# Top-k attention with two MLPs: the weights w3 and w4 prepared first, key and value buffers planned, 28 low halves moved to GpSimd

## The chip, the cores and the metric

The kernel runs on one core of a Trainium2 chip. The metric is device time in microseconds (us), the median of several executions; a profile comes from one further execution.

The engines are named as in the profile: PE is the matrix engine (PEld its weight loads), DVE the vector engine, ACT the scalar engine, POOL GpSimd, and SP the engine whose queue (SPq) issues every DMA of this kernel.

## The reference

Shapes: q, k, v are 4 x 8 heads x 576 x 64 (float32); w_in 512 x 2048, w_out 2048 x 512, w1 and w2 512 x 1024, w3 1024 x 1024, w4 1024 x 512, all float64.

```python
scores = scale * np.matmul(q, k.transpose(0, 1, 3, 2))
kth = np.partition(scores, -32, axis=-1)[..., -32:-31]
scores = np.where(scores >= kth, scores, -1e9)
attn = softmax(scores)
x = np.matmul(attn, v)              # to 2304 tokens x 512
h = x @ w_in
g = np.where(h > 0.0, h, np.exp(np.minimum(h, 0.0)) - 1.0)
x = g @ w_out
out = ((x @ w1) * (x @ w2)) @ w3 @ w4
```

## The kernel before

**Tiling.** The 2304 tokens are cut into nine chunks of 256 (two tiles of 128 tokens). For every chunk `attention` makes x in buffer `XS` (three of them) out of four pairs of heads by two tiles; `mlp` then runs the chunk's matmuls in units: A (w_in, eight units), O (w_out, eight), Y (the evacuation between the MLPs), B (w1 and w2, eight) and D (the product of w3 and w4, one for each tile of tokens). The units of a chunk are written beside the attention of the next one.

**Attention.** For each tile and pair, q and k are split into a high and a low part (`QH`, `QL`; the key buffer `KT` holds both), the scores go through PSUM to `SS`, DVE finds the 32nd largest with four MAX8 and three MATCH_REPLACE8 for each head (L445, L447), ACT makes the exponentials, POOL the low halves (L471), the DMA transposes them (`PT`), PE multiplies by the values (L488), and a second transpose writes x (L510).

**Weights.** The raw words are float64. `load64` brings 128 x 512 words of 64 bits by one DMA and makes float32 of them: ACT (L539), DVE (L540), ACT (L541), POOL (L542). There are 16 such loads for w_in, 16 for w_out, 24 for w3 and w4, and 16 for w1 and w2, 72 in all. `prep_34` multiplies w3 by w4 in float32 (L686), so that D needs one product. Each weight is then normed and `convert` splits every piece into a high and a low float16 half. The high half is ACT's. The low half has a mode: "P" computes it on PE (L578, L579) and evacuates it by a DVE cast (L582); "D" computes it on DVE (L569). Before: w_in and w_out 16 P each, the w3-w4 product 8 D, w1 and w2 16 D.

**Homes.** There is no memory to spare, so raw words and the float32 pieces lie in buffers whose proper content comes later: `RAW8` (the w12 buffer) holds raw words for w_in and w_out, `RAW4` (half of it) those of w3 and w4; four pieces of w_in and four of w_out lie in the w34 buffer, so w34 cannot be filled before they are converted; pieces of w3 lie in `PP`, w4 in the upper half of the w12 buffer, and one piece of the product in the third x buffer.

**Key and value buffers.** `KT` has three and `VV` four, taken in turn. The first use of a batch and pair loads raw keys and splits them (ACT, POOL L358), then stores the split form to DRAM; later uses load that.

**The order.** Every instruction is handed to `Program.op` with an engine, a cost, the buffers that it reads and writes, and a priority. `emit` runs a list schedule once, with the priority (`PAR`, and an offset for each kind of unit and engine in `OFF`) less a multiple of the remaining critical path, and writes the instructions out in that order; the engines then run their queues in order. The order in which the `prep_` functions are called fixes which use of a shared buffer comes first: before, v's norm, w_in, w_out, w3 with w4, w1 with w2.

Of the kernel before, what the change touches and what calls it, by code (L numbers as in the profile page):

```python
# [8 lines left out]
F32 = mybir.dt.float32  # L9
# [24 lines left out]
PAR = dict(hv={}, lv={'wi': 16, 'wo': 16}, whole=(), cd={'wi': [0, 0], 'wo': [0, 0], 'w34': [8, 0], 'w12': [16, 0]}, pv=-577.81, pi=702.591, p34=-453.754, po=123.714, p12=822.408,   # L34
# [5 lines left out]
OFF = {":DVE": 13807, "A0:ACT": -12479, "A0:PE": 9089, "A0:POOL": 28926, "A1:ACT": 1887, "A1:PE": 1481, "A1:POOL": -6842, "A2:ACT": 12564, "A2:PE":  # L40
# [25 lines left out]
       -31006, "att8x:SP": -7783, "attsa:ACT": -35277, "attsa:PE": -26655, "attsk:ACT": -32653, "attsk:POOL": -8699, "attsk:SP": 1080, "attsm:ACT":  # L66
       65030, "attsm:POOL": 51251, "attsp:ACT": -17693, "attsp:POOL": 9395, "attsp:SP": 6312, "attsq:ACT": -8541, "attsq:POOL": 34851, "attsq:SP":
       1875, "attss:ACT": -12797, "attss:PE": -8952, "attst:DVE": 49668, "attsv:ACT": 31908, "attsv:DVE": 21919, "attsv:SP": 16024, "attsx:ACT":
# [3 lines left out]
       "w_in.c:PE": 10958, "w_in.n:DVE": -1688, "w_in.n:PE": 13297, "w_in:ACT": 7341, "w_in:DVE": -15198, "w_in:POOL": -10845, "w_in:SP": -55636,  # L72
       "w_out.c:ACT": -938, "w_out.c:DVE": -15709, "w_out.c:PE": -21068, "w_out.n:DVE": -35012, "w_out.n:PE": -11456, "w_out:ACT": 4851, "w_out:DVE":
       21248, "w_out:POOL": 24755, "w_out:SP": 20119, "w_v0:DVE": -51831, "w_v0:PE": 18056, "w_v0:SP": -23242, "w_v1:DVE": -16660, "w_v1:PE": 25930,
       "w_v1:SP": 54158, "w_v:DVE": -44716}


def conv_modes(n, d, g):

    m = ["P"] * n  # L80
    for k in range(d):
        m[k * n // d] = "D"
    free = [i for i in range(n) if m[i] == "P"]
    for k in range(min(g, len(free))):
        m[free[k * len(free) // g]] = "G"
    return m
# [7 lines left out]
class Program:  # L94
# [30 lines left out]
    def emit(self):  # L125
        n = len(self.ops)
        succ = [[] for _ in range(n)]
        miss = [0] * n
        for i, o in enumerate(self.ops):
            miss[i] = len(o[3])  # L130
            for d in o[3]:
                succ[d].append(i)
        cp = [0.0] * n
        for i in range(n - 1, -1, -1):
            e, c = self.ops[i][:2]
            cp[i] = c + max([cp[s] + (2050.0 if e == "SP" else LAT.get((e, self.ops[s][0]), 130.0)) for s in succ[i]], default=0.0)
        rank = [o[4] - PAR["cpw"] * cp[i] for i, o in enumerate(self.ops)]
# [4 lines left out]
        rt = [0.0] * n  # L142
        for i in range(n):
            if miss[i] == 0:
                heapq.heappush(wait[self.ops[i][0]], (0.0, i))
        order = []
        done, dma, locked = [], 0.0, 0.0
        for _ in range(n):
# [23 lines left out]
            if e == "SP":  # L172

                if len(done) >= 8:
                    t = max(t, done[-8])
                begin = max(dma, t + (1100.0 if lat < 500.0 else 1275.0))
                free[e] = max(t + lat, begin + 131.0) if lat > 1300.0 else t + lat
                dma = begin + cost
                end = dma + (1500.0 if lat > 1300.0 else 1900.0 if lat > 1000.0 else 1100.0)
                done.append(end)  # L180
            else:
                end = free[e] = t + cost
            for s in succ[i]:
                rt[s] = max(rt[s], end + (0.0 if e == "SP" else LAT.get((eng, self.ops[s][0]), 130.0)))
                miss[s] -= 1
                if miss[s] == 0:
                    heapq.heappush(wait[self.ops[s][0]], (rt[s], s))
        order.sort()
# [7 lines left out]
def kernel(ctx: ExitStack, tc: tile.TileContext, qd, kd, vd, vn, w_in, w_out, w1, w2, w3t, w4, out,  # L196
# [532 lines left out]
    def mlp(c, t0, n, dprev, pr0, span, hooks=None):  # L729
# [148 lines left out]
        if dp:  # L878
            seq.append(("Dp", dp.pop(0)))
# [108 lines left out]
```

## Time and profile before

| | |
|---|---|
| median of 3 runs | 1062.55 us (1062.33 to 1064.52) |
| time of the profiled execution | 1063.52 us |
| its span | 1061.7 us |
| busy PE / DVE / ACT / POOL | 978.0 / 888.4 / 826.1 / 695.2 us |
| mean granted PE clock | 0.974 |

The span is the time from the first to the last instruction of the profiled execution; what lies around it is 1.8 us. A busy share counts an engine as busy while one of its instructions runs; the idle time in front of an instruction is put down to what released it.

### The profile page before, as it was taken

What the parts mean: (1) busy time and instruction counts of PE and PEld (TensorE: products, weight loads), DVE (VectorE), ACT (ScalarE), POOL (GpSimd) and SP (SyncE); (2) the same over time, 40 slices, a digit from 0 to 9 for tenths busy, and PEclk for the clock granted to TensorE, in tenths of its full rate; (3) what the DMA queues carried; (4) which work ended last, traced back from release to release, by engine and by line L of the source; (5) the groups of instructions that cost most, each with busy time, mean ns of one, the idle gap of its engine ahead of it and who ended that gap; (6) DMA issues with size and microseconds to landing.
All of it is one profiled execution on the core that took longest, in us unless ns stands there. A gap on an engine that the chain in (4) does not pass through costs nothing.

```text
span 1061.7 us, 24618 instructions
## 1 busy us (share of the span) xinstructions
PE 978.0 (92%) x9132; PEld 776.7 (73%) x9132; DVE 888.4 (84%) x1968; ACT 826.1 (78%) x1521; POOL 695.2 (65%) x743
## 2 busy tenths in 40 slices
PE   3486998988899999999999999999999999999998
PEld 2334454777787788977888888788778968978875
DVE  4999998999999999999979999997999999710011
ACT  6899987898999767978887788899669877824512
POOL 4968665698478646965884587489457856833702
PEclk9598999999999999999999999999999999999999
DMA  9979997689456985488787536865862663320000
GB/s 356 397 223 289 304 273 171 192 209 236 118 161 153 238 192 120 90 193 212 187 227 174 147 76 176 221 188 140 179 154 65 138 151 70 57 51 21 1 20 20
DMA packets 255384, 174.97 MB, mean 165 GB/s; under 512 B 196640, under 2 KB 223264, under 8 KB 255264
## 3 DMA queue, kind: packets, MB, share of 16 engines
q1 hardware_dynamic: 255264, 173.41, 63.2%
q8 instruction: 71, 1.16, 0.5%
q14 instruction: 49, 0.40, 0.1%
HBM read 104.56 MB, written 21.61 MB: 119 GB/s over the span
## 4 chain that ended last, share of the span: by engine, by line
PE 33%; DVE 26%; ACT 16%; DMA 11%; POOL 6%; issue 6%; SPq 1%; DVEq 0%; ACTq 0%; POOLq 0%
DVE m L445 10%; DVE wk L447 8%; PE psR L826 2%; PE psR L827 2%; PE psR L828 2%; PE psY L784 2%; DMA raw<-kd 2%; PE psY L786 2%; PE psY L785 2%; DMA qr<-qd 2%; DMA pt<-pi 2%; PE psR L747 2%; PE psR L748 2%; PE psR L749 2%; PE psY L686 2%
## 5 line engine op out<-in xcount | busy, mean ns | idle before, releaser
L445 DVE MAX8 m<-wk 128x8 f32<-128x576 f32 x432 | 311.2, 746 | 0.8
L471 POOL TENSOR_TENSOR pi<-s,pi 128x576 f16<-128x576 f32 x144 | 185.9, 1298 | 80.3 <-ACT pi L470 57.1
L447 DVE MATCH_REPLACE8 wk<-m,wk 128x576 f32<-128x576 f32 x288 | 212.3, 740 | 0.0
L747 PE MATMUL psR<-x,win 128*128 128x256 f16 x576 | 157.2, 273 | 5.9 <-ACT t L768 5.6
L785 PE MATMUL psY<-g,wout 128*128 128x256 f16 x576 | 158.1, 275 | 3.3 <-POOL g L771 3.3
L784 PE MATMUL psY<-g,wout 128*128 128x256 f16 x576 | 158.5, 275 | 1.1 <-ACT g L770 1.1
L826 PE MATMUL psR<-x,w 128*128 128x256 f16 x576 | 158.0, 274 | 1.2 <-DVE t L846 0.9
L786 PE MATMUL psY<-g,wout 128*128 128x256 f16 x576 | 158.1, 274 | 0.0
L827 PE MATMUL psR<-x,w 128*128 128x256 f16 x576 | 157.6, 274 | 0.0
L828 PE MATMUL psR<-x,w 128*128 128x256 f16 x576 | 157.5, 273 | 0.0
L749 PE MATMUL psR<-x,win 128*128 128x256 f16 x576 | 157.0, 273 | 0.0
L748 PE MATMUL psR<-x,win 128*128 128x256 f16 x576 | 157.0, 273 | 0.0
L435 PE MATMUL psS<-kt,qh 128*128 128x288 f32 x320 | 111.7, 363 | 19.5 <-ACT s L437 18.4
L460 ACT ACTIVATE s<-s,m 128x576 f32<-128x576 f32 x144 | 108.6, 770 | 23.4 <-DVE m L445 23.2
L437 ACT ACTIVATE s<-psS 128x576 f32<-128x576 f32 (+1 forms) x160 | 102.9, 643 | 16.4 <-PE psS L435 9.7
L445 DVE MAX8 m<-s 128x8 f32<-128x576 f32 x144 | 104.5, 744 | 10.5 <-ACT s L437 10.3
L462 ACT ACTIVATE s<-s,ty 128x576 f32<-128x576 f32 x144 | 106.7, 769 | 4.4 <-POOL ty L456 4.4
L447 DVE MATCH_REPLACE8 wk<-m,s 128x576 f32<-128x576 f32 x144 | 106.1, 740 | 0.0
L470 ACT ACTIVATE pi<-s 128x576 f16<-128x576 f32 x144 | 95.0, 676 | 8.7 <-DMA pt<-pi 8.1
L769 POOL TENSOR_TENSOR t<-t,t 128x512 f32<-128x512 f32 x72 | 92.8, 1290 | 5.5 <-ACT t L768 3.8
L415 POOL TENSOR_TENSOR ql<-qr,qh 128x256 fp32r<-128x256 f32 x72 | 54.1, 752 | 60.8 <-ACT qh L414 57.0
L435 PE MATMUL psS<-kt,ql 128*128 128x288 f32 x320 | 93.4, 305 | 0.1
(155 smaller groups left out, 2382.6 us busy)
## 6 DMA issues: line engine op xcount, KB each, us to landing
kt<-kd SPq DMA_DIRECT2D x32, 576.0 KB, 4.6
vv<-vd SPq DMA_DIRECT2D x32, 455.0 KB, 4.6
qr<-qd SPq DMA_DIRECT2D x72, 128.0 KB, 3.0
raw<-kd SPq DMA_DIRECT2D x32, 288.0 KB, 3.8
kd<-kt SPq DMA_DIRECT2D x16, 576.0 KB, 4.6
w<-w_in SPq DMA_DIRECT2D x16, 512.0 KB, 5.9
w<-w_out SPq DMA_DIRECT2D x16, 512.0 KB, 6.9
w<-w3t SPq DMA_DIRECT2D x16, 512.0 KB, 5.5
```

The source lines that it names most:

```text
L435: T.matmul(psS[:, half, 0:288], lhsT=L[qs][:, hh], rhs=KT[kk][:, hh, half * 288:half * 288 + 288], start=li == 0, stop=li == 1)
L445: op("DVE", 665, lambda r=r, src=src, m8=m8, hh=hh: V.max(m8[:, hh, 8 * r:8 * r + 8], src), [skey], [mk], p1 + PAR["ot"] * STEP)
L447: op("DVE", 727, lambda r=r, src=src, w=w, m8=m8, hh=hh: V.match_replace(w, m8[:, hh, 8 * r:8 * r + 8], src, -3.0e38), [skey, mk], [k], p1 ...
L471: op("POOL", 1240, lambda Y=Y, PIs=PIs, hh=hh: G.tensor_tensor(PIs[:, hh, S:2 * S], Y[:, hh], PIs[:, hh, 0:S], op=OP.subtract), hks, [pk], ...
L747: T.matmul(o, lhsT=hi(W)[:, cs], rhs=X[:, 0, kd_, 0:N], start=kd_ == 0, stop=False)
L748: T.matmul(o, lhsT=hi(W)[:, cs], rhs=X[:, 1, kd_, 0:N], start=False, stop=False)
L784: T.matmul(o, lhsT=hi(W)[:, cs], rhs=rh, start=ft == 0 and m % 2 == 0, stop=False, skip_group_check=True)
L785: T.matmul(o, lhsT=hi(W)[:, cs], rhs=rl, start=False, stop=False, skip_group_check=True)
L786: T.matmul(o, lhsT=lo(W)[:, cs], rhs=rh, start=False, stop=ft == 15, skip_group_check=True)
L826: T.matmul(o, lhsT=hi(W)[:, cs], rhs=X[:, 0, kd_, 0:N], start=kd_ == 0, stop=False)
L827: T.matmul(o, lhsT=hi(W)[:, cs], rhs=X[:, 1, kd_, 0:N], start=False, stop=False)
L828: T.matmul(o, lhsT=lo(W)[:, cs], rhs=X[:, 0, kd_, 0:N], start=False, stop=kd_ == 3)
```

## The change

1. The calls are reordered: v's norm, w3 with w4, w_in, w_out, w1 with w2.
2. Raw words and pieces get other homes: raw w_in in the w_out buffer (eight places), raw w3, w4 and w_out in half of the w12 buffer (four places, one ring), v's norm in the upper half of w_in's buffer; four pieces of w_in and one of the product in the `T2` ring, three of w_out in the `GG` ring, both of which the A units write later.
3. A fourth mode "S" makes a low half with two POOL instructions: a scaling in place and a subtraction. `cd` sets 6 of w_in, 6 of w_out, all 8 of the product and 8 of w1 and w2 to S, 28 in all (the short description of the change says 34); 10 of w_in and 10 of w_out stay P and 8 of w1 and w2 stay D.
4. The key and value buffers are planned: a use that finds its content in a buffer loads nothing, the buffer whose next use is farthest is overwritten, and only what is loaded again is stored to DRAM. Odd chunks take the pairs of heads in reverse order.
5. The list schedule runs three times: once as before, then twice more with a rank made by a backward pass over the schedule just found (`fb=2`). All offsets in `OFF` have new values.

Two further options (`blag`, with `bprev` and `hold`) are added and switched off (`blag=0`).

```diff
-PAR = dict(hv={}, ... cd={'wi': [0, 0], 'wo': [0, 0], 'w34': [8, 0], 'w12': [16, 0]}, ...
+PAR = dict(fb=2, snake=1, blag=0, hv={}, ... cd={'wi': [0, 0, 6], 'wo': [0, 0, 6], 'w34': [0, 0, 8], 'w12': [8, 0, 8]}, ...
...
+    for z, mode in ((g, "G"), (s, "S")):
+        free = [i for i in range(n) if m[i] == "P"]
+        for k in range(min(z, len(free))):
+            m[free[k * len(free) // z]] = mode
...
+        cur = self.forward(succ, rank)
+        for _ in range(PAR["fb"]):
+            cur = self.forward(succ, self.backward(succ, cur[2]))
...
+    def pairs(c):
+        return range(4) if c % 2 == 0 or not PAR["snake"] else range(3, -1, -1)
+
+    def plan(n, uses):
...
+                if x in homes:
+                    steps.append((homes.index(x), "hit"))
+                    continue
+                far = [-1 if h in u else len(uses) + n - k if h is None else min([j for j in last[h] if j > i], default=len(uses)) for k, h in enumerate(homes)]
+                k = far.index(max(far))
+                homes[k] = x
+                if x in seen:
+                    again.add(x)
+                steps.append((k, "again" if x in seen else "first"))
+                seen.add(x)
...
     def att_loads(b, p, pr):
-        ks = nxt("k", NK)
-        if ("k", b, p) in seen:
+        ks, how = next(kplan)
+        if how == "hit":
+            return ks
+        if how == "again":
...
-        dma(KD[b, p], KT[ks].rearrange("p a s -> p (a s)").bitcast(F32), 128 * S * 8, [("k", ks)], [("kd", b, p)], pr + PAR["ost"] * STEP)
+        if (b, p) in kagain:
+            dma(KD[b, p], KT[ks].rearrange("p a s -> p (a s)").bitcast(F32), 128 * S * 8, [("k", ks)], [("kd", b, p)], pr + PAR["ost"] * STEP)
...
-    RAW8 = [r64(W12T, "w12", i) for i in range(8)]
-    RAW4 = RAW8[:4]
-    R12 = RAW8[6:]
+    RIN = [r64(WoutT, "wo", i) for i in range(8)]
+    RMID = [r64(W12T, "w12", i) for i in range(4)]
+    R12 = [r64(W12T, "w12", i) for i in (6, 7)]
...
-    HOMES = {"wi": [(W34[i], [("w34", i)]) for i in range(4)], "wo": [(W34[4 + i], [("w34", 4 + i)]) for i in range(4)], "w34": [(EX, ["ex"])], "w12": PPH[2:]}
+    HOMES = {"wi": T2H[:4], "wo": GGH, "w34": [T2H[4]], "w12": PPH[2:]}
...
-        if mode == "G":
-            op("ACT", 570, lambda: A.activation(st, st, AF.Copy, scale=s), [sk], skeys, pr)
+        if mode in "GS":
+            if mode == "G":
+                op("ACT", 570, lambda: A.activation(st, st, AF.Copy, scale=s), [sk], skeys, pr)
+            else:
+                op("POOL", 660, lambda: G.tensor_scalar(st, st, s, 1.0, op0=OP.mult, op1=OP.mult), [sk], skeys, pr)
             op("POOL", 1160, lambda: G.tensor_tensor(lo(W[i]), st, hi(W[i]), op=OP.subtract), [*skeys, (nm, i)], [(nm, i, "l")], pr)
...
     prep_v(0, PAR["pv"] * STEP)
+    prep_34(PAR["p34"] * STEP)
     prep_in(PAR["pi"] * STEP)
     prep_out(PAR["po"] * STEP)
-    prep_34(PAR["p34"] * STEP)
     st12 = prep_12(PAR["p12"] * STEP)
```

## Rows read from the trace of the kernel before

**Rows 1.** The page: busy time of each engine, share of the span, count

```profile
PE 978.0 (92%) x9132; PEld 776.7 (73%) x9132; DVE 888.4 (84%) x1968; ACT 826.1 (78%) x1521; POOL 695.2 (65%) x743
```

**Rows 2.** Busy time by stretch: start:end, length, PE, PEld, DVE, ACT, POOL, clock, DMA

```profile
0.00:195.00 195.00, 147.00 (x713) 78.06 (x714) 177.18 (x377) 164.30 (x292) 128.13 (x129) 0.89 0.93 280
195.00:270.00 75.00, 64.88 (x742) 56.46 (x740) 72.61 (x162) 67.99 (x127) 65.08 (x65) 0.98 0.84 214
270.00:925.00 655.00, 633.09 (x6519) 536.50 (x6517) 625.51 (x1394) 546.67 (x1021) 453.23 (x501) 0.99 0.64 154
925.00:1062.00 137.00, 132.99 (x1167) 105.64 (x1164) 13.14 (x38) 47.17 (x85) 48.81 (x50) 0.99 0.10 23
...
0.00:182.00 182.00, 134.00 (x675) 71.73 (x676) 164.18 (x349) 155.34 (x277) 122.80 (x122) 0.88 0.97 294
```

**Rows 3.** Timeline of PE at the first A unit: start, length, line

```profile
189.58 5.31 PE L686 MATMUL psY<-w,pp 128*128 128x512 f32 x12
194.73 0.27 PE L747 MATMUL psR<-x,win 128*128 128x256 f16 x1
```

**Rows 4.** The line of the last transpose of the first chunk's x: start and landing

```profile
L510 SPq DMA_TRANSPOSE x<-xt x1: 1167/1167/1167, 178.3 to 178.3; - x1
...
DMA to landing us min/median/max: 3.9/3.9/3.9
```

**Rows 5.** The chain that ended last, from 180 to 196 us: start, length, line

```profile
180.11 6.87 PE psY L686 x16
```

**Rows 6.** Low halves in mode P: L582 (shortest/median/longest ns, first to last start); busy time of L578, of L579

```profile
L582 DVE CAST win<-psY x16: 672/684/698, 55.4 to 78.3; 128x512 f16<-128x512 f32 x16
L582 DVE CAST wout<-psY x16: 667/682/692, 96.3 to 121.5; 128x512 f16<-128x512 f32 x16
...
0.00:195.00 195.00, 38.24 (x64) 11.14 (x64) 0.89 0.93 280
...
0.00:195.00 195.00, 12.85 (x32) 3.30 (x32) 0.89 0.93 280
```

**Rows 7.** Groups of DVE instructions by line, from 0 to 182 us: busy, mean ns

```profile
L445 DVE MAX8 m<-wk 128x8 f32<-128x576 f32 x60 | 43.9, 749 | 0.0
L540 DVE SCALAR_TENSOR_TENSOR w<-w,psR 128x512 int32<-128x512 int32 x56 | 37.5, 679 | 4.5 <-ACT psR L539 4.5
```

**Rows 8.** POOL lines: mode S's nearest, and the conversion of raw words

```profile
L762 POOL TENSOR_SCALAR t<-t,sc x72: 687/695/1284, 201.4 to 1001.5; 128x512 f32<-128x512 f32 x72
...
L771 POOL TENSOR_TENSOR g<-t,g x72: 1151/1163/1465, 205.7 to 1008.6; 128x512 f16<-128x512 f32 x72
...
L542 POOL TENSOR_TENSOR wout<-wout,w x12: 1288/1296/1307, 44.1 to 72.7; 128x512 int32<-128x512 int32 x12
```

**Rows 9.** SP's queue: first and last load of w1 and w2's sixteen

```profile
192.35 0.34 SPq L288 DMA_DIRECT2D pp<-w  x1
...
256.34 0.53 SPq L288 DMA_DIRECT2D pp<-w  x1
```

**Rows 10.** DVE: low halves in mode D and a top-k line; last the mean, 250 to 302

```profile
L569 DVE SCALAR_TENSOR_TENSOR w<-w,sc x21: 729/751/2698, 257.3 to 297.3; 128x512 f16<-128x512 f32 x21
...
L447 DVE MATCH_REPLACE8 wk<-m,wk x288: 730/741/756, 27.2 to 921.1; 128x576 f32<-128x576 f32 x144
...
L569 DVE SCALAR_TENSOR_TENSOR w<-w,sc 128x512 f16<-128x512 f32 x21 | 21.5, 1046 | 0.2
```

**Rows 11.** DMA issues by line: count, size, median us to landing

```profile
kt<-kd SPq DMA_DIRECT2D x32, 576.0 KB, 4.6
vv<-vd SPq DMA_DIRECT2D x32, 455.0 KB, 4.6
...
kd<-kt SPq DMA_DIRECT2D x16, 576.0 KB, 4.6
...
vd<-vv SPq DMA_DIRECT2D x16, 455.0 KB, 4.8
```

**Rows 12.** What PE waited for from 270 to 925 us: total, times, longest

```profile
PE psA L488 <- DMA pt<-pi: 7.4, 8, 2.2
```

More of the change, by code (lines that the diff above doesn't have):

```diff
@@ L123, in op, with forward @@
         self.groups.append(f"{self.tag}:{eng}")
-    def emit(self):
+    def forward(self, succ, rank):
         n = len(self.ops)
[L127 to L137, printed above, removed]
+        miss = [len(o[3]) for o in self.ops]
         engs = sorted({o[0] for o in self.ops})
@@ L142, in emit @@
         rt = [0.0] * n
+        fin = [0.0] * n
         for i in range(n):
@@ L182, in emit @@
                 end = free[e] = t + cost
+            fin[i] = end
             for s in succ[i]:
@@ L187, in emit, with backward @@
                     heapq.heappush(wait[self.ops[s][0]], (rt[s], s))
+        return max(free.values()), order, fin
+    def backward(self, succ, fin):
+        n = len(self.ops)
+        miss = [len(s) for s in succ]
+        engs = sorted({o[0] for o in self.ops})
+        free = {e: 0.0 for e in engs}
+        wait = {e: [] for e in engs}
+        ready = {e: [] for e in engs}
+        rt = [0.0] * n
+        late = [0.0] * n
+        for i in range(n):
+            if miss[i] == 0:
+                heapq.heappush(wait[self.ops[i][0]], (0.0, i))
+        for _ in range(n):
+            best = None
+            for e in engs:
+                if ready[e]:
+                    t = free[e]
+                elif wait[e]:
+                    t = max(free[e], wait[e][0][0])
+                else:
+                    continue
+                if best is None or t < best[0]:
+                    best = (t, e)
+            t, e = best
+            while wait[e] and wait[e][0][0] <= t:
+                _, i = heapq.heappop(wait[e])
+                heapq.heappush(ready[e], (-fin[i], i))
+            _, i = heapq.heappop(ready[e])
+            eng, cost, fn, deps, pr, lat, lk = self.ops[i]
+            free[e] = t + (max(cost, lat) if e == "SP" else cost)
+            end = free[e] + (1100.0 if e == "SP" else 0.0)
+            late[i] = -end
+            for d in deps:
+                de = self.ops[d][0]
+                rt[d] = max(rt[d], end + (900.0 if de == "SP" else LAT.get((de, eng), 130.0)))
+                miss[d] -= 1
+                if miss[d] == 0:
+                    heapq.heappush(wait[de], (rt[d], d))
+        return late
@@ new lines, in emit @@
+    def emit(self):
+        n = len(self.ops)
+        succ = [[] for _ in range(n)]
+        for i, o in enumerate(self.ops):
+            for d in o[3]:
+                succ[d].append(i)
+        cp = [0.0] * n
+        for i in range(n - 1, -1, -1):
+            e, c = self.ops[i][:2]
+            cp[i] = c + max([cp[s] + (2050.0 if e == "SP" else LAT.get((e, self.ops[s][0]), 130.0)) for s in succ[i]], default=0.0)
+        rank = [o[4] - PAR["cpw"] * cp[i] for i, o in enumerate(self.ops)]
+        cur = self.forward(succ, rank)
+        for _ in range(PAR["fb"]):
+            cur = self.forward(succ, self.backward(succ, cur[2]))
+        self.length, order, _ = cur
@@ L188, in emit @@
         order.sort()
-        self.length = max(free.values())
-        self.busy = {e: sum(o[1] for o in self.ops if o[0] == e) for e in engs}
+        self.busy = {e: sum(o[1] for o in self.ops if o[0] == e) for e in {o[0] for o in self.ops}}
         for _, i in order:
@@ L344 @@
     op("DVE", 135, consts, [], ["ident", ("xf", 0), *[(k, i) for k in ("v", "vl") for i in range(NV)]], -1e6)
+    def pairs(c):
+        return range(4) if c % 2 == 0 or not PAR["snake"] else range(3, -1, -1)
+    def plan(n, uses):
+        last, homes, seen, again, steps = {}, [None] * n, set(), set(), []
+        for i, u in enumerate(uses):
+            for x in u:
+                last.setdefault(x, []).append(i)
+        for i, u in enumerate(uses):
+            for x in u:
+                if x in homes:
+                    steps.append((homes.index(x), "hit"))
+                    continue
+                far = [-1 if h in u else len(uses) + n - k if h is None else min([j for j in last[h] if j > i], default=len(uses)) for k, h in enumerate(homes)]
[5 more added lines that the diff above has]
+                seen.add(x)
+        return iter(steps), again
+    starts = [sum(chunks[:i]) for i in range(len(chunks))]
+    kuse, vuse = [], []
+    for c_, n_ in enumerate(chunks):
+        for p_ in pairs(c_):
+            for t_ in range(starts[c_], starts[c_] + n_):
+                kuse.append([(b_, p_) for b_ in range(t_ * 128 // S, (t_ * 128 + 127) // S + 1)])
+            vuse.append([(b_, p_) for b_ in sorted({starts[c_] * 128 // S, ((starts[c_] + n_) * 128 - 1) // S})])
+    kplan, kagain = plan(NK, kuse)
+    vplan, vagain = plan(NV, vuse)
     def att_loads(b, p, pr):
-        ks = nxt("k", NK)
-        if ("k", b, p) in seen:
+        ks, how = next(kplan)
+        if how == "hit":
+            return ks
+        if how == "again":
             dma(KT[ks].rearrange("p a s -> p (a s)").bitcast(I32), KD[b, p].bitcast(I32), 128 * S * 8, [("kd", b, p)], [("k", ks)], pr)
             return ks
-        seen.add(("k", b, p))
         for hh in range(2):
@@ L400, in attention @@
         Kc, Vc = {}, {}
-        for pair in range(4):
-            base = (t0 * 8 + pair * n * 2 + PAR["a0"] * (c == 0) + PAR["a1"] * (c == 1)) * STEP
+        for at, pair in enumerate(pairs(c)):
             for t in range(n):
                 gt = t0 + t
-                idx = t0 * 8 + (pair * n + t) * 2
+                idx = t0 * 8 + (at * n + t) * 2
                 pr = (idx + PAR["a0"] * (c == 0) + PAR["a1"] * (c == 1)) * STEP
@@ L544 @@
     PPH = [(PP[:, 2 * i:2 * i + 2].rearrange("p a b -> p (a b)"), [("pp", 2 * i), ("pp", 2 * i + 1)]) for i in range(4)]
-    EX = XS[2].rearrange("p e k n -> p (e k n)").bitcast(F32)[:, 0:512]
-    HOMES = {"wi": [(W34[i], [("w34", i)]) for i in range(4)], "wo": [(W34[4 + i], [("w34", 4 + i)]) for i in range(4)], "w34": [(EX, ["ex"])], "w12": PPH[2:]}
+    T2H = [(T2[i], [("t", i)]) for i in range(NT2)]
+    GGH = [(GG[i], [("gh", i), ("gl", i)]) for i in range(NG)]
+    HOMES = {"wi": T2H[:4], "wo": GGH, "w34": [T2H[4]], "w12": PPH[2:]}
     def home(W, nm, i, n=16):
@@ L591, in prep_v @@
             if b == 0:
-                dst, keys = W12T[:, 2 * i:2 * i + 2].rearrange("p a b -> p (a b)")[:, 0:S], [("w12", 2 * i), ("w12", 2 * i + 1)]
+                dst, keys = WinT[:, 8 + 2 * i:10 + 2 * i].rearrange("p a b -> p (a b)")[:, 0:S], [("wi", 8 + 2 * i), ("wi", 9 + 2 * i)]
             else:
@@ L648, in prep_out @@
         P.tag = "w_out"
-        st = [stage(Wout, "wo", i, w_out[i * 128:i * 128 + 128, :], pr + i * PAR["pos"] * STEP, RAW8) for i in range(16)]
+        st = [stage(Wout, "wo", i, w_out[i * 128:i * 128 + 128, :], pr + i * PAR["pos"] * STEP, RMID) for i in range(16)]
         P.tag = "w_out.n"
@@ L669, in prep_34 @@
         for k in range(8):
-            load64(W4[k][0], W4[k][1], w4[k * 128:k * 128 + 128, :], None, pr, RAW4, "w34", "w4" in PAR["whole"])
+            load64(W4[k][0], W4[k][1], w4[k * 128:k * 128 + 128, :], None, pr, RMID, "wo", "w4" in PAR["whole"])
         def part(m):
@@ L726, in finish_12, with mlp @@
                 for i in range(16)]
-    def mlp(c, t0, n, dprev, pr0, span, hooks=None):
+    def mlp(c, t0, n, dprev, pr0, span, hooks=None, bprev=(), hold=False):
         xs, vb = c % NXS, batch(t0 + n)
@@ L877, in mlp @@
         dp = list(dprev)
+        seq += [("Bp", b) for b in bprev]
         if dp:
@@ L882, in mlp @@
             seq.append(("Dp", dp.pop(0)))
-        for j in range(8):
-            seq.append(("B", j))
+        if not hold:
+            for j in range(8):
+                seq.append(("B", j))
         for kind, i in seq:
             pr = pr_of(u)
-            c_ = c - (kind == 'Dp')
+            c_ = c - (kind in ("Dp", "Bp"))
             P.tag = f"{kind[0]}{c_ if c_ < 4 or c_ > len(chunks) - 3 else chr(115)}"
@@ L900, in mlp @@
                 i(pr)
-                u += 1
+                u += kind == "Dp"
             u += kind != "Y"
-        return [lambda pr, t=t: unitD(t, pr) for t in range(n)]
-    starts = [sum(chunks[:i]) for i in range(len(chunks))]
+        ds = [lambda pr, t=t: unitD(t, pr) for t in range(n)]
+        return (ds, [lambda pr, j=j: unitB(j, pr) for j in range(8)]) if hold else ds
     prep_v(0, PAR["pv"] * STEP)
+    prep_34(PAR["p34"] * STEP)
     prep_in(PAR["pi"] * STEP)
     prep_out(PAR["po"] * STEP)
-    prep_34(PAR["p34"] * STEP)
     st12 = prep_12(PAR["p12"] * STEP)
+    done12 = []
     def hooks(kind, i):
-        if kind == "Y":
+        if not done12 and (kind == "Bp" or kind == "Y" and not PAR["blag"]):
+            done12.append(1)
             for f in finish_12(st12, (PAR["p12"] + 16 * PAR["p12s"]) * STEP):
                 f()
-    dprev = []
+    dprev, bprev = [], ()
     for c, n in enumerate(chunks):
@@ L929 @@
             banks[:] = [0, 1] if c == 1 else [0, 1, 2]
-            dprev = mlp(c - 1, starts[c - 1], m, dprev, (starts[c] * 8 + PAR["lag0" if c == 1 else "lag"]) * STEP, m * 8 * STEP, hooks if c == 1 else None)
+            banks[:] = [0, 1] if c == 1 + PAR["blag"] else banks
+            hold = c == 1 and PAR["blag"] == 1
+            dprev = mlp(c - 1, starts[c - 1], m, dprev, (starts[c] * 8 + PAR["lag0" if c == 1 else "lag"]) * STEP, m * 8 * STEP, hooks if c < 3 else None, bprev, hold)
+            bprev = ()
+            if hold:
+                dprev, bprev = dprev
     c = len(chunks) - 1
```

48 lines of the change are left out of this document (22 added, 26 removed), and 56 rows, old and new, of the table OFF.

## The prediction

> **What bounds the kernel now.** I read the page first, then the busy time by stretch, then the places where one stretch ends. On the page PE is busy for 978.0 of 1061.7 us and DVE for 888.4 [rows 1]; a share over the whole span hides that the two are full at different times, so the stretches decide. Until 195 us PE works 147.0 of 195 us while DVE works 177.2: DVE is the fullest engine there. From 195 to 270 PE idles 10.1 us, from 270 to 925 it idles 21.9 of 655, and from 925 to the end 4.0 of 137, with DVE nearly idle [rows 2]. So the top-k is over 137 us before the end while PE still owes that much matmul time: PE is behind, and the end is *the start of the first A unit, plus PE's work from there, plus PE's idle time from there*. In numbers: 194.7 + 831 + 36 = 1061.7; the 831 is 978.0 less the 147.0 done by then. None of the 831 is preparation on PE that the change takes away: the P pieces were all done by 122 us [rows 6], and the other weights used D. The change can act on the first term and the third.
>
> What starts the first A unit? It begins at 194.7 directly behind the last product of w3 with w4 [rows 3], while the last piece of the first chunk's x was issued at 178.3 and landed 3.9 later, at 182.2 [rows 4]. So 12.5 us of the first term are PE finishing w3 times w4 in front of A; the rest is the pace of the first chunk's attention and the weights, which DVE, ACT and POOL share.
>
> **The change part by part.**
>
> *Order of the weights.* The product of w3 and w4 costs PE 128 half products; a dense run of 16 took 6.87 us, 0.43 each [rows 5], so 55 us in all. They ran up to 194 us, in front of A, and move to the first hundred microseconds, where PE idles for want of work. That alone is worth the 12.5 us to x's landing. More needs an earlier x: DVE loses 12 casts in front of it, 12 x 0.68 = 8.2 us [rows 6], so 174 at best.
>
> The condition is that w_in and w_out, now behind 24 more loads, are ready too: A reads w_in, and A's results go to the `GG` buffers that hold three pieces of w_out. I bound that from two sides. By load on the engines: what has to be done before A is nearly the list of before, 164.2 us of DVE, 155.3 of ACT and 122.8 of POOL by 182 [rows 2], less 8.2 on DVE, plus 20 S pieces on POOL. An S costs 0.70 + 1.16 = 1.86 us by the nearest rows [rows 8], so 37 us: DVE 156, ACT 155, POOL 160. All three come out alike; at the 90% that DVE held (164.2 / 182), POOL is through at 178, and at the 87% that POOL itself held in its busiest stretch (65.1 of 75 [rows 2]) at 184. By pace: the last of twelve pieces of w_out was finished at 74.0 [rows 8], the 28th load of the order w_in, w_out, so 2.64 each, 56 by 148; w_out's casts began 22 us behind that row and lasted 25 [rows 6]: 195. I take 180, nearer the first, since before the 28 loads by 74 shared their engines with loads of w4: DVE had handled 56 of all weights by 182 beside 60 MAX8 [rows 7]. That is **minus 14.7** (bounds minus 20.7 with A at 174, and 0 at 195).
>
> *P to S, 12 pieces.* On PE a P piece took (38.24 + 12.85) / 32 = 1.60 us [rows 6], so 19 us of PE work go. They lie before the first A, where PE idles 48 us: counted at **nothing**. If PE became full there, they would be worth those 19.
>
> *D to S, 16 pieces, and the stretch of w1 and w2.* DVE made its low halves in mode D at 257 to 300 us at a mean of 1.05 [rows 10]; 16 fewer, 17 us, leave a stretch in which DVE is full (72.6 of 75) and the first B waits on them. POOL gets 8 x 1.86 = 14.9 on top of 65.1 of 75: 80, five too many, unless w1 and w2 come earlier. They can: their first load was issued at 192.4 [rows 9], since w3's and w4's places were not free before; now these wait only for w_out's words. But ahead of A POOL is at 88% already, and up to 270 us it would have 128.1 + 65.1 + 28 x 1.86 = 245 us, 91%; only the second chunk's attention can give way. DVE's relief and POOL's burden cancel: **0** (bounds minus 10, PE's whole idle time in this stretch, and plus 9, POOL's 245 us at 88%).
>
> The median D took 0.75 us but the mean 1.05 and the longest 2.70, while 288 MATCH_REPLACE8 stayed within 730 to 756 ns beside the same POOL [rows 10]; so more POOL work costs the top-k nothing. The Trainium skill, "SBUF — State Buffer", section "Who interferes with whom", says that a DVE instruction with two SBUF inputs and a GpSimd instruction that reads SBUF contend for a shared read port, and the one that comes second is blocked for the whole instruction. The rows agree: D reads the piece and its high half. By the rule at its worst, with the top-k in that class too, 28 x 1.86 = 52 us of POOL would be taken from DVE and the forecast would become slower; the narrow MATCH_REPLACE8 row speaks against that, and I put it at 2 in 100, within the last rival.
>
> *Planned keys and values.* Stepping through `plan` over the nine chunks gives 12 loads of split keys for 32, 6 of values for 32, 12 stores of keys for 16 and 6 for 16 [rows 11]: 60 DMAs fewer and (20 + 4) x 0.576 + (26 + 10) x 0.455 = 30 MB less, on the queue in which the transposes stand. PE waited 7.4 us for these in 270 to 925 [rows 12]; the other 14 us of idle time there are waits on ACT and POOL, spread thin.
>
> *Three passes of the schedule, new offsets, reversed pairs.* No row prices an order. Beneath, 21.9 us of idle time can go; above, a worse order adds. Together with the loads I take **minus 5** for 270 to 925 (bounds minus 14 and plus 8).
>
> *The sum.* 1061.7 - 14.7 - 0 - 5 = 1042.0 for the span. The profiled execution took 1063.52, 1.8 more than its span, and stands 1.0 above the median of 1062.55; the median is 0.85 above that span. So **1043 us**, and 1028 to 1056 if the mechanism holds (first A at 174 to 190, the other terms between half their bounds).
>
> **The rivals.**
>
> *More than that* (1006 to 1028). PE's idle time after the first A, 36 us, is larger than the first term's gain, and DVE's 25 us of relief (17 + 8) lie where it was full. With the first A at 174 and the 36 cut to 18 the span is 1061.7 - 20.7 - 18 = 1023. Against it: 14 us of that idle time are waits of a microsecond or so each, which no single edit meets. Chance 0.13.
>
> *The start is hidden anyway* (1056 to 1064). The weights take the place of w3 times w4 as what A waits for, at the 195 of the slower pace: the first term gives nothing and the small ones 0 to minus 5. For it: w_out has four raw places instead of eight, in one ring with w3 and w4. Against it: the dense loads of before were paced by full engines, not by places. Chance 0.11.
>
> *Slower: POOL sets the start* (1064 to 1082). POOL's 160 us in front of A need 88% of the time; up to 182 it reached 67%. Its place is the last low halves of w_out, behind raw words, keys and probabilities in one queue; they hold back the `GG` buffers and so every A. At 80% POOL is through at 200, at 75% at 213: the first A is 5 to 18 late, and plus 0 to 2 for the rest. It decides from some 82% (160 / 195) down. Against it: POOL idled in front of A because ACT or DVE handed it work late, and some of its work by 182 is the second chunk's, which can wait. Chance 0.14.
>
> **How the numbers follow.** The forecast has 0.62. A change within 0.2% (1060.4 to 1064.7) is about what a measurement of this kernel cannot tell from none. Faster: 0.62 + 0.13 + 0.06 of the hidden start; within 0.2%: the other 0.05; slower 0.14. The range leaves out the slower rival (0.14) and the lower part of the better one (0.05): 1014 to 1063.
>
> **What would show it.** In the changed kernel's profile the w3-w4 products lie before 110 us; the first w_in matmul is at 174 to 190, not behind L686; L582 counts 20, the D line 8, a POOL scaling in place 28 at 0.7 us; kt<-kd counts 12 and vv<-vd 6; POOL is above 80% busy in front of the first A; PE is idle some 50 us before it and under 36 behind it; PE's busy time falls by 13 to 19 (13 at the dense rate of rows 5). The prediction is wrong if the first A stays at 190 or later, or if PE's idle time behind it moves by more than the start does: then the order was worth more than the starting point.

## The result, and the profile after

The changed kernel takes 1052.6 us (1052.16 to 1056.5, 4 runs), the kernel before 1062.4 beside it: a ratio of 0.9914 (0.9885 to 0.9942). It is faster by 9 us where 20 were forecast. The profiled execution took 1056.5 us with a span of 1054.7.

The page, the same rows as in [rows 1] and [rows 11], and the forty slices of PE:

```profile
PE 963.5 (91%) x9096; PEld 772.1 (73%) x9096; DVE 878.5 (83%) x1940; ACT 826.0 (78%) x1521; POOL 743.2 (70%) x799
PE   2598775697999999999999999999999999999998
...
kd<-kt SPq DMA_DIRECT2D x12, 576.0 KB, 4.2
kt<-kd SPq DMA_DIRECT2D x12, 576.0 KB, 3.9
...
vd<-vv SPq DMA_DIRECT2D x6, 455.0 KB, 4.7
vv<-vd SPq DMA_DIRECT2D x6, 455.0 KB, 4.5
```

PE lost 14.5 us of work, POOL gained 48, the DMAs are the counted ones, but DVE lost only 10 us of work where 25 were counted on. The products of w3 and w4 and the first A and B units (shortest/median/longest ns, first to last start), and the stretches up to the first A, to the first B, and to the end, as in [rows 2]:

```profile
L771 PE MATMUL psY<-w,pp x128: 590/592/1220, 40.8 to 120.5; 128*128 128x512 f32 x128
...
L832 PE MATMUL psR<-x,win x576: 269/273/421, 209.3 to 997.7; 128*128 128x256 f16 x192
...
L911 PE MATMUL psR<-x,w x576: 269/273/286, 283.1 to 1040.1; 128*128 128x256 f16 x192
...
0.00:209.30 209.30, 141.29 (x750) 76.92 (x751) 185.87 (x394) 180.90 (x322) 171.36 (x173) 0.90 0.88 267
209.30:283.10 73.80, 64.72 (x690) 57.77 (x688) 73.41 (x146) 63.83 (x119) 66.36 (x70) 0.91 0.48 107
283.10:1054.70 771.60, 757.51 (x7665) 637.37 (x7662) 619.27 (x1402) 581.22 (x1082) 505.45 (x558) 1.00 0.45 104
```

The products did move to the front and are over at 120 us. Yet the first A comes at 209.3, 14.6 us *later* than before, and the first B at 283.1, 13 later; PE idles 68.0 us ahead of A instead of 48. All of that is made good behind it. A cut at a fixed time shows where; PE's busy time up to 300 us and behind it, before, then after:

```profile
0.00:300.00 300.00, 238.34 (x1684) 157.53 (x1685) 279.36 (x598) 259.95 (x468) 207.07 (x207) 0.91 0.85 247
300.00:1061.70 761.70, 739.62 (x7450) 619.13 (x7448) 609.09 (x1371) 566.18 (x1055) 488.18 (x537) 1.00 0.55 132
```

```profile
0.00:300.00 300.00, 222.42 (x1614) 149.11 (x1615) 274.49 (x576) 259.83 (x468) 253.85 (x260) 0.91 0.78 221
300.00:1054.70 754.70, 741.10 (x7488) 622.95 (x7484) 604.05 (x1365) 566.12 (x1054) 489.31 (x540) 1.00 0.44 103
```

At 300 us both kernels have the same matmul work left, 739.6 and 741.1 us. The changed one has done 15.9 less by then, about what the change took away, and idled 15.9 more (77.6 for 61.7). So the start gained nothing, and the difference of 7 us between the two spans is idle time behind 300 us: 22.1 before, 13.6 after. The profiled execution of the changed kernel is the longest of its four, and the medians differ by 9.8; where the other 3 us lie, these two profiles do not show. Of PE's waits behind 300 us, those for transposes [rows 12] went from 7.4 to 1.0:

```profile
PE psS L516 <- ACT s L518: 2.0, 4, 1.1
...
PE psA L569 <- DMA pt<-pi: 1.0, 2, 0.6
```

### The profile page after: what moved, and what is told of

The parts are those of the page before. It is cut to its first block, busy times and chain, and to the rows that moved or that the text cites. A ratio compares the mean times of both kernels' runs of the same rounds, so it can differ in the third digit from the quotient of the medians.

```text
span 1054.7 us, 24477 instructions
## 1 busy us (share of the span) xinstructions
PE 963.5 (91%) x9096; PEld 772.1 (73%) x9096; DVE 878.5 (83%) x1940; ACT 826.0 (78%) x1521; POOL 743.2 (70%) x799
## 4 chain that ended last, share of the span: by engine, by line
PE 31%; DVE 29%; ACT 14%; POOL 6%; DMA 5%; issue 5%; SPq 0%; POOLq 0%; ACTq 0%; DVEq 0%
DVE m L526 13%; DVE wk L528 10%; PE psR L911 3%; PE psR L913 3%; PE psR L912 3%; PE psR L832 2%; PE psR L834 2%; PE psR L833 2%; PE psY L869 2%; PE psY L871 2%; PE psY L870 2%; DMA qr<-qd 2%; PE psS L516 2%; PE psA L569 2%; ACT s L543 2%
## 5 line engine op out<-in xcount | busy, mean ns | idle before, releaser
L551 ACT ACTIVATE pi<-s 128x576 f16<-128x576 f32 x144 | 97.3, 685 | 7.6 <-DMA pt<-pi 7.4
L516 PEld LDWEIGHTS psS<-kt,qh 128*128 128x128 f32 x320 | 62.9, 196 | 42.6 <-ACT s L518 21.4
```

Source lines behind the costliest of these rows:

```text
L516: T.matmul(psS[:, half, 0:288], lhsT=L[qs][:, hh], rhs=KT[kk][:, hh, half * 288:half * 288 + 288], start=li == 0, stop=li == 1)
```

## The experiments

Theories: the order of the weights and the modes set the start (the prediction's); the fewer transfers count; the three passes of the schedule count; or only the offsets, chosen for this one program. All ratios are to the kernel before.

**One part undone, planned anew.** Each time the schedule is made again with the offsets of the changed kernel. e1 puts the turn-taking `plan` of the kernel before in place of the new one, e4 restores the homes and order of the weights.

```diff
-    kplan, kagain = plan(NK, kuse)          # e1: buffers in turn, all stored
-PAR = dict(fb=2, ...                        # e2
+PAR = dict(fb=0, ...
-cd={'wi': [0, 0, 6], 'wo': [0, 0, 6], 'w34': [0, 0, 8], 'w12': [8, 0, 8]}   # e3
+cd={'wi': [0, 0], 'wo': [0, 0], 'w34': [8, 0], 'w12': [16, 0]}
-    prep_34(...)                            # e4: behind prep_out again
```

> The changed kernel with key and value buffers taken in turn again (32 loads of split keys, 32 of values, everything stored), all else as changed. If the fewer transfers are what moved the time, PE's waits for the transposed probabilities behind the first B, 1.0 us, go back to about 7 and the time to 1059 or more. If the order made the gain, the time stays within 2 us of 1052.6, since the order is planned anew around the added transfers.

> The changed kernel with one pass of the list schedule instead of three, offsets as changed. If the order is what moved the time, PE's idle time behind the first A, 23 us, grows to 36 or more and the time to 1062 or more. If transfers or the order of the weights made the gain, the time stays below 1056.

> The changed kernel with the modes of before: no low half by POOL, 32 by PE and 24 by DVE. If POOL's 52 us of low halves are what keeps the first A back at 209, it comes at 195 or sooner, and the time falls to 1045 or is at least no higher. If moving them to POOL helped, by 17 us less of DVE and 19 us less of PE in front of A, the first A comes later than 209 and the time is 1057 or more.

> The changed kernel with the weights in the order and the homes of before (w_in, w_out, then w3 and w4), modes and key buffers as changed. If w3 and w4 first is worth what the prediction said, some 15 us at the first A, the time is 1062 or more. If the order of the weights only moves the wait from PE to POOL, ACT and DVE, the time is within 4 us of 1052.6.

| | ratio (95%) | first A, first B | PE work, idle |
|---|---|---|---|
| changed kernel | 0.9914 (0.9885 to 0.9942) | 209, 283 | 963.5, 91.2 |
| e1, buffers in turn | 0.9958 (0.9935 to 0.9981) | 218, 284 | 966.1, 93.1 |
| e2, one pass | 1.0190 (1.0147 to 1.0233) | 229, 296 | 975.5, 110.0 |
| e3, modes of before | 1.0051 (1.0030 to 1.0072) | 180, 267 | 972.3, 89.2 |
| e4, weights as before | 1.0044 (1.0016 to 1.0072) | 193, 282 | 970.4, 97.6 |

The last two columns are those of the profiled execution alone; that of e3 is the shortest of eleven, 6.7 us below their median. Read by the ratios, e1, e3 and e4 would be worth 5 to 15 us each and e2 29, far more together than 9. e3 is the telling one: without POOL's low halves the first A comes at 180.0, as the prediction had it, and the kernel is slower than before. An early first A did not bring an early end.

**What an order alone does.** The same program with offsets moved at random by at most 1500:

```diff
-OFF = {":DVE": 19917, "A0:ACT": -36723, ...
+OFF = {each of them + randint(-1500, 1500)}
```

> The changed kernel with every offset of the schedule moved by a random amount of at most 1500 (they differ from those of before by some 15000), nothing else. It shows what a new order alone does to the time. If the offsets are a fine optimum for this one program, the time rises by 5 us or more, and the runs that undo one part and plan anew cannot be read below that; if it stays within 2 us, a loss of 7 us or more in those runs is due to the part undone.

> The changed kernel with another random draw of offsets moved by at most 1500. If the first draw, 0.9999, is typical, the ratio to before is 0.996 or more; if it was bad luck, 0.990 to 0.995.

> The kernel before, one pass, with its offsets moved by at most 1500 at random. If offsets found for one program are worth some 9 us in any kernel of this kind, the ratio is 1.005 to 1.015, and the changed kernel keeps its lead at drawn offsets. If the kernel before loses nothing, the changed kernel's gain is its offsets alone.

Measured: 0.9999 (0.9983 to 1.0014) and 1.0074 (1.0053 to 1.0094) for two draws of the changed kernel, 1.0043 (1.0019 to 1.0066) for one of the kernel before. A small push of the offsets costs the changed kernel 9 to 17 us, all of its gain and more, and the kernel before 5. It also moves the first A, from 209.3 to 190.7 and 190.9, with every part of the change in place. So e1, e3 and e4, which also run at offsets not chosen for them, cannot be read as the worth of the part undone: e3 and e4 lie between the two draws, and e1 on the good side of them. Only e2 is slower than both.

**One part alone, on the kernel before.**

```diff
+    def plan(n, uses): ...                  # e5: planned buffers, old sequence of pairs
+PAR = dict(fb=2, ...                        # e6, e12: forward() and backward(), old offsets
+tiny(... V.tensor_scalar ...)               # g2: e6 with the edit of e7, below
```

> The kernel before with only the planned key and value buffers (pairs in the old sequence), one pass, old offsets. If fewer transfers give the gain, PE's waits for transposes, 7.4 us from 270 to 925, fall to about 1 and the time to 1055. If the order does, the time is within 3 us of 1062.5.

> The kernel before with only the three passes of the schedule, old offsets. If the two backward passes give the gain, PE's idle time behind the first A falls from 36 to about 23 us and the time to 1052 to 1056. If the gain needs the offsets that were found for it, the time is 1060 or more.

> The kernel before with three passes of the schedule and the same random draw of offsets as e11 (1.0043 with one pass). If the passes gain at any offsets, the ratio is 0.992 to 0.998. If the gain of e6 (0.9916) was luck of its offsets, 1.000 or more.

> The kernel before with three passes of the schedule and the tiny tensor_tensor as tensor_scalar, the order as in e6. There these instructions take some 0.5 to 0.7 us each, 7 us in all, for 3 if they are not held up. If weights, modes and planned buffers add nothing at their chosen offsets, the ratio is 0.986 to 0.990, as for the changed kernel with the same mend (0.9857); if they add, 0.991 or more.

The planned buffers alone: 1.0789 (1.0747 to 1.0831), neither of the two outcomes named, with 140 us of PE idle time and 18.9 us of waits for transposes between 300 and 1060 us; why one pass places the planned loads so badly was not followed further. The passes alone: 0.9916 (0.9888 to 0.9943), the gain of the whole change; at drawn offsets 0.9901 (0.9881 to 0.9920), against 1.0043 for the same draw with one pass. With the edit of g2 0.9908 (0.9890 to 0.9927): DVE has 7 us less to do than in e6, and the time is the same. That lies between the two outcomes named, and is read below, beside e7. Here are e6 and e12, cut at 300 us:

```profile
0.00:300.00 300.00, 239.31 (x1693) 157.82 (x1694) 284.56 (x600) 261.77 (x471) 208.56 (x207) 0.97 0.85 248
300.00:1053.80 753.80, 736.02 (x7441) 617.18 (x7439) 606.88 (x1369) 562.64 (x1051) 486.24 (x536) 1.00 0.56 133
```

```profile
0.00:300.00 300.00, 239.46 (x1712) 158.51 (x1713) 283.58 (x604) 263.33 (x474) 209.75 (x209) 0.98 0.86 247
300.00:1047.10 747.10, 732.90 (x7423) 615.88 (x7420) 604.25 (x1365) 560.32 (x1048) 485.21 (x535) 1.00 0.55 135
```

They have 3.6 and 6.7 us less work left at 300 us than the kernel before, and 17.8 and 14.2 us of idle time behind it for 22.1. Together that is 7.9 us behind 300 us in e6, about what the changed kernel saves there (7.0), without a change of weights, modes or buffers; but only half of it is idle time. The 14.6 of e12 are too many: its profiled execution is the shortest of five, 5 us below their median.

**Transfers at the same order, and w1 and w2 held back.** f4 issues a transfer that nobody reads behind sixty of the loads of q, with the planner's input unchanged. e8 makes the loads of w1 and w2 wait for the first x and calls their preparation behind the first attention; its order is planned anew, with the offsets of the changed kernel.

```diff
+                    Q.dma_start(DUM[d % 4][:, 0:S], kd[d % 4, d % 8])           # f4
-        dma(st, src, 128 * 512 * 8, [], rk, pr)                                 # e8
+        dma(st, src, 128 * 512 * 8, [("xh", 0, k) for k in range(4)] if nm == "w12" else [], rk, pr)
-    st12 = prep_12(PAR["p12"] * STEP)
+    st12 = []
...
+        if c == 0:
+            st12 += prep_12(PAR["p12"] * STEP)
```

> The changed kernel in the same order with one more transfer of 288 KB (keys from DRAM to DRAM, into a scratch tensor that nothing reads) behind each load of q from the thirteenth on: 60 more DMAs, as many as the plan of the key and value buffers took away, with 17 MB read and 17 written. If transfers were worth the gain, PE's waits for transposes, 1.0 us, rise to 5 or more and the time by 4 us or more. If they lie beside other work, less than 2 us.

> The changed kernel with the sixteen loads of w1 and w2 held until the first chunk's x has landed. In the changed kernel they run at 105 to 207 us, in front of the first A, where before they ran at 192 to 256. If they are what keeps the first A back at 209, with 21 us on POOL, 20 on ACT and 11 on DVE, it comes at 195 or sooner; the first B, then behind them, at 285 or later, and the time is the same or up to 5 us more. If the low halves on POOL keep A back, A stays near 209.

f4: 0.9970 (0.9952 to 0.9988), 6 us more than the changed kernel; PE's waits for transposes behind 300 us are 3.0 for 1.0, its idle time there 17.6 for 13.6. The time moved as if transfers were worth the gain, the waits did not. Sixty transfers cost some 6 us, then (2 to 10 by the two intervals), though little of it shows as a wait. They are not the ones that the plan took away: those were 576 and 455 KB, between DRAM and SBUF; and each of the sixty also takes a place in SP's queue, which was not separated from its bytes. e8: 0.9970 (0.9949 to 0.9990); the first A comes at 189.2, the first B at 303.2. Holding the loads of w1 and w2 brings A forward by 20 us and puts B back by 20. But as in e3 the order is a new one, and the draws above bring A to 191 with these loads about where they were; so this does not show that the loads alone had pushed A back.

**Which engine sets the start.** The same instructions in the same order, some of them on 16 columns: the 28 scalings of mode S (f1), 26 of the MAX8 (f2), 26 of the exponentials (f3), planned as 16 to 17 us less for one engine each.

```diff
+ G.tensor_scalar(st[:, 0:16], st[:, 0:16], s, 1.0, op0=OP.mult, op1=OP.mult)      # f1
+ V.max(m8[:, hh, 8 * r:8 * r + 8], src[:, 0:z])                # f2: z = 16, tiles 6 to 18, r = 3
+ A.activation(Y[:, hh, 0:z], Y[:, hh, 0:z], AF.Exp, ...)       # f3: z = 16, tiles 6 to 18
```

> The changed kernel, same instructions in the same order, with the 28 scalings on POOL done on 16 columns instead of 512 (part of the scaling is left out): 28 x 0.6 = 17 us less of POOL, all between 130 and 302 us, 20 of them in front of the first A. If POOL sets the start, PE's idle time in the first 300 us, 77.6, falls by 8 or more and the time by 6 to 14 us. If DVE sets it, the time falls by less than 3 us, except for what DVE waits for POOL.

> The changed kernel, same instructions in the same order, with the last MAX8 of 26 rows of the top-k (tiles 6 to 18) on 16 of 576 scores (part of the top-k is left out): 26 x 0.6 = 16 us less of DVE, most of it between 100 and 260 us. If DVE sets the start, PE's idle time in the first 300 us falls by 8 or more and the time by 6 to 14 us. If POOL or ACT sets it, the time falls by less than 3 us.

> The changed kernel, same instructions in the same order, with 26 of the exponentials (tiles 6 to 18) on 16 of 576 columns (part of the exponentials is left out): 26 x 0.6 = 16 us less of ACT over the same stretch. If ACT sets the start, the time falls by 6 to 14 us; if DVE or POOL does, by less than 3 us. If all three engines share it, each of the three runs gives 2 to 6 us.

f1 0.9859 (0.9835 to 0.9883), f2 0.9874 (0.9852 to 0.9897), f3 0.9917 (0.9889 to 0.9945): 6, 4 and 0 us less than the changed kernel, the 4 only just clear of noise. The engines' busy time over the run fell by less than planned, 11.3 us on POOL (f1), 11.9 on DVE (f2), 9.9 on ACT (f3), and PE's idle time in the first 300 us by 3.6, 3.5 and not at all, where 8 or more had been named. The gain shows as work done by then: 734.9 (f1), 733.5 (f2) and 742.0 us (f3) are left at 300 us for 741.1.

The order was the same, but the three are not clean: DVE instructions with two inputs in SBUF (the memory that DVE and POOL work in) change their length from run to run. In f1 DVE's own busy time fell from 878.5 to 871.4 with no DVE instruction changed, and two instructions on 128 x 1 numbers make 6.4 of these 7.1 us; e7 below gains as much by mending them alone. So f1 shows no worth of POOL's work beyond them. In f2 and f3 the same two were short as well, but one low half of the values was long (timeline, start and length; the changed kernel, f2, f3):

```profile
234.78 0.98 DVE L467 SCALAR_TENSOR_TENSOR vv<-raw,sc,vv 128x640 f16<-128x640 f32 x1
...
230.64 7.15 DVE L467 SCALAR_TENSOR_TENSOR vv<-raw,sc,vv 128x640 f16<-128x640 f32 x1
...
239.24 6.27 DVE L467 SCALAR_TENSOR_TENSOR vv<-raw,sc,vv 128x640 f16<-128x640 f32 x1
```

There the two changes nearly cancel, and the 4 us of f2 speak for DVE's other work; ten us less of ACT gave nothing.

**The tiny instructions.** In the changed kernel two DVE operations on 128 x 1 numbers last four microseconds (timeline, start and length):

```profile
238.10 3.77 DVE L694 TENSOR_TENSOR sc<-sc 128x1 f32<-128x1 f32 x1
241.80 0.75 DVE L526 MAX8 m<-wk 128x8 f32<-128x576 f32 x1
242.47 0.14 DVE L695 RECIPROCAL sc<-sc 128x1 f32<-128x1 f32 x1
242.53 4.44 DVE L702 TENSOR_TENSOR sc<-sc 128x1 f32<-128x1 f32 x1
```

POOL was busy without a break beside them; these are its instructions beside the second one, which ended at 246.97, with the last but one of them:

```profile
242.63 1.16 POOL L856 TENSOR_TENSOR g<-t,g 128x512 f16<-128x512 f32 x1
243.75 1.28 POOL L552 TENSOR_TENSOR pi<-s,pi 128x576 f16<-128x576 f32 x1
244.99 0.74 POOL L498 TENSOR_TENSOR ql<-qr,qh 128x256 fp32r<-128x256 f32 x1
245.68 1.28 POOL L854 TENSOR_TENSOR t<-t,t 128x512 f32<-128x512 f32 x1
247.04 1.42 POOL L441 TENSOR_TENSOR kt<-raw,kt 64x576 fp32r<-64x576 f32 x1
```

e7 writes such lines with one column as a scalar operand; b1 also issues the scalings of mode S on ACT, at the same places.

```diff
-        tiny(lambda: V.tensor_tensor(phi, sv, r, op=OP.mult), ...       # e7, b1: eight such lines
+        tiny(lambda: V.tensor_scalar(phi, sv, r, None, op0=OP.mult), ...
-                op("POOL", 660, lambda: G.tensor_scalar(st, st, s, 1.0, op0=OP.mult, op1=OP.mult), ...    # b1
+                op("POOL", 660, lambda: A.activation(st, st, AF.Copy, scale=s), ...
```

> The changed kernel with its eight lines of tiny DVE tensor_tensor on two 128x1 columns in SBUF written as tensor_scalar with the second column as the scalar; the same order of instructions. Two of these took 3.77 and 4.44 us at 238 to 247 us, beside a POOL that is full. If they wait for POOL because they have two SBUF inputs, each becomes 0.2 us, DVE gains 8 us in front of the first B, which comes up to 7 earlier, and the time falls by 2 to 7 us. If something else stretched them, they stay long and the time is the same.

> The changed kernel with the tiny instructions as tensor_scalar and the 28 scalings issued on ACT, at their places in the order, instead of on POOL; everything is computed. If DVE and POOL set the start and ACT has room (16 us less of ACT gave nothing), the gains of 6 us each add in part, since both free the same DVE instructions: ratio to before 0.980 to 0.985. If ACT then becomes the bound, 28 x 0.6 = 17 us more on it, 0.986 or more.

e7: 0.9857 (0.9824 to 0.9891), 1050.1 us, the fastest version here that computes everything, beside 0.9914 for the changed kernel. The same two operations in e7, and in f1, with the POOL instructions beside them in f1:

```profile
244.49 0.20 DVE L694 TENSOR_SCALAR sc<-sc 128x1 f32<-128x1 f32 x1
245.28 0.14 DVE L695 RECIPROCAL sc<-sc 128x1 f32<-128x1 f32 x1
245.34 0.19 DVE L702 TENSOR_SCALAR sc<-sc 128x1 f32<-128x1 f32 x1
```

```profile
240.34 1.10 DVE L694 TENSOR_TENSOR sc<-sc 128x1 f32<-128x1 f32 x1
242.09 0.66 DVE L702 TENSOR_TENSOR sc<-sc 128x1 f32<-128x1 f32 x1
...
240.15 1.27 POOL L854 TENSOR_TENSOR t<-t,t 128x512 f32<-128x512 f32 x1
241.44 1.29 POOL L552 TENSOR_TENSOR pi<-s,pi 128x576 f16<-128x576 f32 x1
```

In f1 POOL is as full there as in the changed kernel (17.8 of the 18 us from 232 on in both), yet each of the two was held for one POOL instruction, not for several. How long such an instruction is held is thus a matter of how it falls between POOL's, and not of POOL's load alone. In e7 the two are short beside a busy POOL, but a low half of the values takes 5.63 us instead; over the run DVE's busy time fell by 7.7.

With the tiny instructions mended the changed kernel stands at 0.9857 and the kernel of before with three passes at 0.9908 (g2), some 5 us apart, the two intervals just touching. So at offsets chosen for it the changed kernel may be ahead; whether by its other parts or by these offsets, the runs do not separate.

b1: 0.9905 (0.9880 to 0.9931), nothing beyond the changed kernel: ACT, 180.9 us busy ahead of the first A in the changed kernel, is at 191.6 of 212.0 there. That 10 us less of ACT gave nothing (f3) did not mean that 16 more are free.

## Why the prediction was off by half

*The order of the weights, minus 14.7: this step failed.* The products of w3 and w4 did leave A's path (over at 120.5 us, 110 was said), and the 12.5 us between x and A went with them: A began 1.0 us behind x. But the first A came at 209.3 and not at 180, because x itself, put at 182.2 or sooner, came at 208.3. (A at 190 or later was the sign of being wrong that the prediction had named.) Its last transpose, as in [rows 4]:

```profile
L591 SPq DMA_TRANSPOSE x<-xt x1: 1191/1191/1191, 206.0 to 206.0; - x1
...
DMA to landing us min/median/max: 2.3/2.3/2.3
```

The step took what lies in front of A to be "nearly the list of before" plus 37 us on POOL: DVE 156, ACT 155, POOL 160. Measured up to the first A: 185.9, 180.9 and 171.4. Part of the excess is w1 and w2, whose loads moved ahead of A, as these lines of SP's queue show (before: 192 to 256 us [rows 9]): of the 72 conversions of raw words on DVE 71 were done by then, where the count of before was 56 [rows 7].

```profile
105.56 0.38 SPq L337 DMA_DIRECT2D pp<-w  x1
...
207.26 0.53 SPq L337 DMA_DIRECT2D pp<-w  x1
```

The sentence on w1 and w2 even said that some would, and did not charge A for it: 15 x 1.3 = 20 us of POOL, and their share of ACT and DVE. e8, which holds them back, has A at 189; e3, with no S, at 180.0. But the two draws, with S and with these loads issued at about the same times (108 to 209 and 104 to 219 us), have A at 190.7 and 190.9 too; here the first:

```profile
L832 PE MATMUL psR<-x,win x576: 269/273/437, 190.7 to 1004.8; 128*128 128x256 f16 x192
```

So the excess in front of A is measured; which of its parts has to move for an earlier x stays open. (The argument for 180 from DVE's pace also read too little: beside the 56 weights DVE had done 82 MAX8 by 182, not 60; [rows 7] is one of two groups.)

*The frame behind that step failed too.* The end was written as the first A, plus PE's work from there as a fixed 831 us, plus idle time. It came out as 209.3 + 822.2 + 23.2: the start 14.6 later, the work 9 less, the idle time 13 less. The work is not fixed, because preparation and attention move across the first A. e3 (A at 180), e8 (189) and both draws (191) are slower than the changed kernel (209). What can be compared is PE's work left at one fixed time behind the start, and at 300 us that is the same before and after.

*DVE's relief was largely taken back.* Counted: 8 + 17 = 25 us less for DVE. Measured: 10 less over the run. The casts and mode D did give 23.5; the tiny instructions took 6 more than before, the two blocked ones among them, and the low halves of the values 3.4 (1.05 us each before and 1.26 after on average). The prediction looked at the top-k beside POOL, rightly (MATCH_REPLACE8 still takes 0.74 us), and at mode D, and missed the small ones. The Trainium skill, "SBUF — State Buffer", section "Who interferes with whom", describes it: a `tensor_tensor` with both inputs in SBUF contends with GpSimd's reads, and an instruction with at most one SBUF input does not, outside the modes in which DVE uses both of its ports. The runs agree: 3.77 and 4.44 us beside a full POOL, 1.10 and 0.66 in f1 beside a POOL as full, 0.2 as `tensor_scalar`. Beyond these 6 us of e7, f2 speaks for DVE's other work, with 4 us for 12 us less of it.

*P to S, counted at nothing: right.* PE's work fell by 14.5 us, within the 13 to 19 named, and its idle time in the first 300 us rose by 15.9. *D to S and w1, w2, counted at 0:* PE's idle time between A and B is 9.1 for 10.1, but the whole stretch lies 14 us later.

*270 to 925, minus 5: right in sign, the term was about half the size.* Idle time behind 300 us fell by 8.5. In the two profiles it was the only gain of the change. The passes alone gain as much time (e6, e12), about half of it as idle time behind 300 us and half as work done by then, and the transfers have a part of their own (f4, some 6 us), which the prediction gave no price. How the two share the 8.5 is not separated: they were not measured at one common order.

*The rival that POOL sets the start* had the right time, A at 200 to 213, but not the right place: it had A held by the last low halves of w_out, and the last of these was made at 216.6, behind the first A, which followed x. f1, with 11 us less of POOL, left A at 210.4. Its price was wrong too: a late A was not paid for at the end.

*What the other parts are worth.* With the passes and drawn offsets the kernel of before stands at 0.990, the changed one at 1.000 and 1.007. Only at its chosen offsets does the changed kernel come back to 0.991. So as the change stands, weights first, S and planned buffers together gain nothing over the passes that these runs can show; with the tiny instructions mended, e7 is ahead of g2 by some 5 us, at the edge of noise. Two draws are few, and whether other offsets would let these parts pay stays open.

## What to carry to other kernels

Where several engines are full, an early start of one unit is not a gain: compare how much work the bounding engine has left at a fixed time after the start, and charge a moved step with everything that moves along with it. Before an undone part is read as its worth, measure what a random push of the order does to the same program; here it was as large as the whole change, and only runs at an unchanged order could be read. Write small DVE arithmetic on columns with a scalar operand instead of two SBUF inputs when GpSimd is busy: it gained 6 us in the changed kernel and cost nothing in g2, where it gained none. And look for such held instructions before a run at an unchanged order is read: their lengths differ from run to run by several us.

## What was not expected of the hardware

A DVE instruction on 128 x 1 numbers lasted 4.44 us beside a GpSimd that was busy without a break, and 0.2 us with one input as a scalar. At the same order of instructions another one with two SBUF inputs, a low half of the values, took 0.98, 5.63, 6.27 or 7.15 us. Sixty transfers of 288 KB between DRAM addresses, which no instruction waits for, cost some 6 us, though PE's recorded waits for transposes rose by only 2.
